# Weight blocks prepared one pair earlier, and layer one's first chains issued within attention

## The chip, the cores and the metric

One core of a Trainium2 chip runs the whole kernel. The metric is the device time of one execution in microseconds (us). Engines: TensorE (PE, matmuls), ScalarE (ACT), VectorE (DVE), GpSimd (POOL), and SyncE (SP), on whose queue all the transfers of this kernel are issued, in order.

## The reference

Causal attention with a decay, then two feed-forward layers, all in float32:

```python
scores = q @ k.T / 8 + cum[:, None] - cum[None, :]      # causal; cum = cumsum(log f)
x = softmax(scores) @ v                                  # 4 batches, 8 heads, 576 tokens, 64 wide
h = x @ w_in;  x = (h * cos(h)) @ w_out                  # 2304 x 512, hidden 2048
g = x @ w_gate; x = (g * sigmoid(g) * (x @ w_val)) @ w_out2   # hidden 1536
```

## The kernel before

Everything is unrolled, and each engine runs its instructions in program order. A matmul that needs float32 is done in three passes over rounded parts: high x high, low x high, high x low. So each weight block becomes a high and a low half, and so does each left operand.

**Attention.** The 32 heads go in 16 pairs. An order written out by hand, `SCH`, is run once per round `n`; an entry such as `N0b@2` runs operation `N0` for pair b (odd) of round `n - 2`. `S` are score matmuls (`S4` those of the last 64 tokens, both pairs of a round together), `M` adds the mask and takes the maximum on DVE, `E` is the exponential on ACT, `T` transposes on PE, `C` copies the transposed tile out of PSUM (ACT, or DVE for `C1`), `V` is the product with v, `N` (L531) multiplies by the reciprocal sums on DVE, `xo` stores the pair's result. `ld` loads a pair's q and k (576 KB, L303) into a ring of `RWB` tiles; `lv` loads v; `r` operations form the reciprocals and send them through DRAM. `XH` places three early products of layer one, `ahead(0..2)`, among the last pair's operations: `h` for hidden blocks 0, 1 and 2 of the first token chunk.

**Weight blocks.** `order` lists the blocks of 128 x 512 float64-wide words (512 KB) in the order of their use. `wd` loads block `i - 1` at pair `i` (L152), and `w1` to `w7` convert it: `w1` absolute value on ACT (L168), `w2` clamp on POOL, `w3` to `w5` shifts and merges on DVE (L172, L174, L176), `w6` and `w7` the high and low half on POOL. The first `SA` = 15 blocks (0 to 14) are done so within attention, on a ring of three raw tiles; block 14 belongs to pair 15. Four further raw tiles are loaded near the end of attention, behind `rf` of pair 15, and worked on within layer one.

**Layer one** goes over six chunks of 384 tokens and 16 hidden blocks, 96 steps. Each step runs the letters of `ORD1` = "0c152cw64cowwc": `0` twelve matmuls into h (L253), `1` n = round(h / 2 pi) on ACT (L665), `2` r = h / 2 pi - n on DVE (L667), `4` the sine on ACT (L669), `5` of the step before: product h * r on DVE (L671) and rounding to gh on ACT (L673), `6` of the step before: gl = h - gh on DVE, `w` weight work, `o` the twelve matmuls of gh and gl two steps back into four accumulator banks (L689, and L692 for the last hidden block of a chunk), `c` a piece of the second layer's weight work. After a chunk's last hidden block `o` also empties the banks: four copies on ACT (L699), or for the two chunks that are split into two halves four sums on DVE (L697). The accumulators are two tiles of two banks (`t_tile`, a ring of two), the same ring that holds attention's transposes and products.

At the seam the program order on each engine is: all of attention, then the steps of layer one from step 0 on. `h` of blocks 0 to 2 exists by then; n, r, the sine, gh and gl do not.

Of the kernel before, what the change touches and what calls it, by code (L numbers as in the profile page):

```python
# [9 lines left out]
F32 = mybir.dt.float32  # L10
F32R = mybir.dt.float32r
I32 = mybir.dt.int32
I64 = mybir.dt.int64
# [7 lines left out]
NPAIR = NH // 2  # L21
# [8 lines left out]
SA = 15  # L30
LAG = 2
PB = 6
RWB = 4
VTB = 3
PTB = 2
PST = 2
WARM = 2
TAB = 2
TAB2 = 6
RWB2 = 4  # L40
HIB = 4
CHAIN = 1
WHE = 1

XH = {("T2", 14): 0, ("T1", 15): 1, ("V0", 15): 2}
SCH = "xka@2 E21a@1 N0a@2 M11b@1 xoa@2 M10b@1 wdb@2 E00a@1 E31a@1 E01a@1 w5b@3 E30a@1 raa@1 lva@1 C3b@2 rba@1 S0b@1 T0b@2 E11b@1 wda@1 S2b@1 M01b@1 w6b@3 T2b@2 rta@1 lda@-1 S3b@1 M20b@1 M21b@1 C0b@2 C2b@2 rca@1 rda@1 E21b@1 M00b@1 M30b@1 T3a@1 M31b@1 E01b@1 w3a@2 V0b@2 w4a@2 S4@0 V1b@2 E00b@1 M40@0 E20b@1 w5a@2 w7b@3 S0a@0 M41@0 N0b@2 E30b@1 xkb@2 w6a@2 C3a@1 E31b@1 T0a@1 ldb@-1 S1a@0 M00a@0 N1b@2 rea@1 rfa@1 xob@2 E10b@1 E40@0 S2a@0 w1b@2 rab@1 rbb@1 C0a@1 E41@0 M10a@0 T2a@1 rtb@1 T1a@1 M01a@0 w7a@2 C2a@1 rcb@1 rdb@1 M11a@0 M20a@0 S3a@0 C1a@1 T1b@1 V0a@1 V1a@1 lvb@1 M21a@0 w1a@1 M30a@0 M31a@0 E11a@0 w2b@2 w3b@2 S1b@0 C1b@1 w4b@2 w2a@1 qs@-1 T3b@1 N1a@1 reb@1 rfb@1 E10a@0 E20a@0"
START = "S2a M21a M20a S3a M31a E20a M30a E21a E31a qs E30a S1a S0a M01a M00a M10a M11a E11a S4 M40 E10a M41 T1a E00a E01a C1a T0a"
DVC = ((1, 0), (1, 1))
JS = 9
# [14 lines left out]
GSUM0 = ((3, 0), (4, 1), (5, 2), (6, 3))  # L64
HAT0, LAT0 = (3, 4, 5, 6, 7, 8, 8), (4, 5, 6, 7, 8, 9, 9)
SEAM = {1: (2, 3), 6: (3, 4), 5: (4, 5), 2: (5, 6), 7: (6, 7), 3: (7, 8), 4: (8, 9)}
ORD1 = "0c152cw64cowwc"
WQ = (3, 2)
NS = 2
WS = 2  # L70
# [27 lines left out]
def body(ctx: ExitStack, tc: tile.TileContext, qk, v, f, w_in, w_out, w_gate, w_val, w_out2, mask_c, ident_c, sel_c, out):  # L98
# [48 lines left out]

    def w_load(n):
        kind, j = order[n]
        sp = stages[0] if n < SA else wraws  # L150
        raw = sp.tile([128, 512], I64, tag="wraw", name="wraw", bufs=3 if n < SA else RWB2)
        SP.dma_start(out=raw, in_=srcs[kind][j])  # L152
        wcur[n] = [raw, None]

# [122 lines left out]
    rctx = ExitStack()  # L277
    xpools[0] = rctx.enter_context(tc.tile_pool(name="xpool", bufs=1, side=SIDE_R))
    wraws = rctx.enter_context(tc.tile_pool(name="wraws", bufs=RWB2, side=SIDE_R))
    actx = ExitStack()  # L280
    ap1 = actx.enter_context(tc.tile_pool(name="ap1", bufs=1))
    ident = ap1.tile([128, 128], F32, name="ident")
# [267 lines left out]
    def op(o, q):  # L550

        if not 0 <= q < NPAIR // 2:
            return
        l = {"a": 0, "b": 1}.get(o[-1])
        if l is not None:
            o, q = o[:-1], 2 * q + l
        if (o, q) not in done:
            done.add((o, q))
            if (o, q) in XH:
                ahead(XH[o, q])  # L560
            act(o, q)
            if (o, q) == ("C0", NPAIR - 1):
                ACT.activation(out=sinp, in_=hpi, func=AF.Sin)
            if (o, q) == ("rf", NPAIR - 1):
                for k in range(RWB2):
                    w_load(SA + k)

    def act(o, i):
        k, e = o[0], int(o[-1]) if o[-1] in "01" else 0
        p = 2 * i + e  # L570
        if o[:2] == "ld":
            i > 1 and load_pair(i)
        elif o == "lv":
            prep_v(i)
        elif o == "S4":
            emit_s4(i)
        elif o[:2] == "M4":
            emit_m4(i, e)
        elif o[:2] == "E4":
            emit_e4(i, e)  # L580
        elif k == "S":
            emit_s(i, int(o[1]))
        elif k == "M":
            emit_m(p, int(o[1]))
        elif k == "E":
            emit_e(p, int(o[1]))
        elif k == "T":
            emit_t(i, int(o[1]))
        elif k == "C":
            emit_c(i, int(o[1]))  # L590
        elif k == "r":
            emit_recip(i, o[1])
        elif k == "V":
            emit_pv(i, e)
        elif k == "N":
            emit_n(i, e)
        elif o == "xo":
            emit_o(i)
        elif o == "xk":
            if i == XL:  # L600
                load_chunk(0, True)
            elif i >= XP:
                for _ in range(min(XN, len(xsplit))):
                    split_x(*xsplit.pop(0))
        elif o == "wd":
            i and w_load(i - 1)
        elif k == "w":
            i and w_step(i - 1, int(o[1]))
        elif o == "qs":
            emit_b(i)  # L610
        else:
            raise ValueError(o)
# [15 lines left out]
        mm_in(h, wt["i", j], xs[0])  # L628

    pools, hs = {}, {}  # L630
    moff = max(int(o) for _, o in sch)
    for o in START.split():
        op(o, 0)
    for n in range(NPAIR // 2 + moff):
        for o, off in sch:
            op(o, n - int(off))
    gsrc[0] = const.tile([1, 1], F32, name="gs")
    pool_round(gsrc[0], rsb[NPAIR - 1][0:1, 0:1])
    actx.close()
    wpools[1] = ctx.enter_context(tc.tile_pool(name="wb", bufs=1))  # L640
    lctx = ExitStack()
    xpools[1] = lctx.enter_context(tc.tile_pool(name="xpool2", bufs=1))
    pp = lctx.enter_context(tc.tile_pool(name="pp", bufs=1))
    mp2 = lctx.enter_context(tc.tile_pool(name="mp2", bufs=1, reuse_waits="tile"))
    mp3 = lctx.enter_context(tc.tile_pool(name="mp3", bufs=3, reuse_waits="tile"))
    stages[1] = rctx.enter_context(tc.tile_pool(name="stage2", bufs=TAB2, side=SIDE_R))
    G = {}
    acc = {}
    part = {}
    loaded = set()  # L650
    hnr = {}

    def in1(c, j, k):

        if k == 0:
            h = hs.pop((c, j), None)
            if h is None:
                h = pools["h"].tile([128, 512], F32, tag="h", name="h")[:, :CH]
                mm_in(h, wt["i", j], xs[c])
            n = mp2.tile([128, CH], I32, tag="n", name="n")  # L660
            r = mp2.tile([128, CH], F32, tag="r", name="r", bufs=2)
            hnr[c, j] = h, n, r
        h, n, r = hnr[c, j]
        if k == 1:
            ACT.activation(out=n, in_=h, func=AF.Copy, scale=INV2PI, bias=0.25)  # L665
        elif k == 2:
            DVE.scalar_tensor_tensor(out=r, in0=h, scalar=INV2PI, in1=n, op0=ALU.mult, op1=ALU.subtract)  # L667
        elif k == 4:
            ACT.activation(out=r, in_=r, func=AF.Sin, bias=hpi, scale=float(2 * np.pi))  # L669
        elif k == 5:  # L670
            DVE.tensor_tensor(out=h, in0=h, in1=r, op=ALU.mult)  # L671
            gh, gl = G[c, j] = [mp3.tile([128, CH], F32R, tag=a, name=a) for a in ("gh", "gl")]
            ACT.copy(out=gh, in_=h)  # L673
        elif k == 6:
            gh, gl = G[c, j]
            subtract(DVE, gl, h, gh)
            del hnr[c, j]

    def out1(g, j):
        c, a, b = SEG[g]  # L680
        gh, gl = G.pop((c, j))
        wo = wt["o", j]
        if j == a:
            for m in range(0, KD, 2):
                t = t_tile()
                acc[m], acc[m + 1] = t[:, 0], t[:, 1]
        for n, (q, x) in enumerate(((0, gh), (1, gh), (0, gl))) if j < b - 1 else ():
            for m in range(KD):
                PE.matmul(acc[m][:, :CH], lhsT=wo[:, q, 128 * m:128 * m + 128], rhs=x, start=(j == a and n == 0), stop=False)  # L689
        for m in range(KD) if j == b - 1 else ():  # L690
            for n, (q, x) in enumerate(((0, gh), (1, gh), (0, gl))):
                PE.matmul(acc[m][:, :CH], lhsT=wo[:, q, 128 * m:128 * m + 128], rhs=x, start=False, stop=(n == 2))  # L692
        if j == b - 1:
            o = part.pop(g)
            for m in range(KD):
                if a:
                    DVE.tensor_tensor(out=o[:, m], in0=acc[m][:, :CH], in1=o[:, m], op=ALU.add)  # L697
                else:
                    ACT.copy(out=o[:, m], in_=acc[m][:, :CH])  # L699
            SP.dma_start(out=x2[c], in_=o)  # L700

    steps = [(g, j) for g, (c, a, b) in enumerate(SEG) for j in range(a, b)]
    wpos = [SA, 2]
# [62 lines left out]
    for i in range(NCH + LAG):  # L766
        if i < NCH:
# [6 lines left out]
            if j == J1 - 7 and c + 1 not in loaded or c == 0 and j == 2 and 1 not in loaded:  # L774
                loaded.add(c + 1)
                load_chunk(c + 1, later=True)
            if i == WS:
                w_step(SA, 1)
            left = WQ[SB <= wpos[0] < SB + 24 and i % 2] if i >= WS else 0
            now[0] = i  # L780
            for k in ORD1:
                if k in "01234":
                    in1(c, j, int(k))
                elif k in "56" and i:
                    in1(SEG[steps[i - 1][0]][0], steps[i - 1][1], int(k))
                elif k == "w" and left:
                    left -= 1
                    w_next()
                elif k == "o" and i >= LAG:
                    out1(*steps[i - LAG])  # L790
                elif k == "c" and small and small[0][0] <= i:
                    small.pop(0)[1]()
            if xsplit and i >= XS:
# [309 lines left out]
```

## Time and profile before

| | |
|---|---|
| median of 3 runs (lowest, highest) | 965.83 us (965.19, 967.13) |
| the profiled execution, its own time | 966.51 us |
| its span, first to last instruction | 964.7 us |
| mean granted TensorE clock | 0.992 |
| PE busy | 944.1 us, 98% |
| DVE, ACT, POOL busy | 717.9, 510.0, 414.5 us |

Times below are from the span's start. Attention fills about the first 160 us, layer one runs to about 566, the second layer to the end. A busy PE counts pipelined matmuls; a granted clock of 1.0 is 2.4 GHz, one of 0.5 is 1.2 GHz.

### The profile page before, as it was taken

Reading aid. Unit: us, or ns where it says so; the run is one execution under the profiler, and the core shown is the slowest. Engines: PE = TensorE matmul, PEld = TensorE weight load, DVE = VectorE, ACT = ScalarE, POOL = GpSimd, SP = SyncE. Lnnn points to the kernel's source line nnn. Section 1 sums busy time; section 2 is a strip of 40 time slices with the busy share of each in tenths; the row PEclk is TensorE's granted clock in tenths of the full one; section 3 lists DMA queues with packets and bytes.
Section 4 is the critical chain, followed back from the end, with each engine's and each line's share of the span. In section 5 each row is a group of like instructions: output and inputs, shape, how many; then the busy total and the mean of one; then the engine's idle time right before and its main releaser. Section 6 shows DMA issues by size and latency. Waiting matters only on the chain.

```text
span 964.7 us, 17731 instructions
## 1 busy us (share of the span) xinstructions
PE 944.1 (98%) x6442; PEld 881.8 (91%) x6442; DVE 717.9 (74%) x1267; ACT 510.0 (53%) x1105; POOL 414.5 (43%) x389
## 2 busy tenths in 40 slices
PE   7999996999999999999999999999999999999998
PEld 4667774999999999999999999999999999988888
DVE  6788885777788788779966535766758585898884
ACT  7999993555655556556555432323324132464552
POOL 1245745423265687597791005545446455000000
PEclk9999998999999999999999999999999999999999
DMA  5577655342467759679847772326841429953431
GB/s 194 196 252 266 220 177 177 99 136 95 153 220 228 249 168 317 206 219 297 270 151 261 252 273 88 116 58 236 307 123 50 123 71 391 346 169 129 134 109 45
DMA packets 108983, 182.60 MB, mean 189 GB/s; under 512 B 8920, under 2 KB 72800, under 8 KB 108896
## 3 DMA queue, kind: packets, MB, share of 16 engines
q1 hardware_dynamic: 108896, 181.47, 56.8%
q8 instruction: 51, 0.84, 0.4%
q14 instruction: 36, 0.29, 0.1%
HBM read 118.44 MB, written 62.99 MB: 188 GB/s over the span
## 4 chain that ended last, share of the span: by engine, by line
PE 82%; DVE 5%; POOL 4%; DMA 4%; ACT 2%; issue 2%; SPq 0%; POOLq 0%; ACTq 0%; DVEq 0%
PE h L253 16%; PE t L689 15%; PE b L874 12%; PE c L874 8%; PE a L874 8%; PE b L963 5%; PE t L522 4%; PE a L963 3%; PE sB L386 2%; PE t L472 2%; DMA xl<-x 2%; PE c L963 2%; PE d L963 2%; PE sA L386 1%; PE t L692 1%
## 5 line engine op out<-in xcount | busy, mean ns | idle before, releaser
L253 PE MATMUL h<-xh,w 128*128 128x384 f32 x768 | 149.0, 335 | 0.0
L689 PE MATMUL t<-gh,w 128*128 128x384 f32 x704 | 138.4, 337 | 9.8 <-ACT gh L673 8.9
L253 PEld LDWEIGHTS h<-xh,w 128*128 128x128 f32 x768 | 134.4, 188 | 0.2
L689 PEld LDWEIGHTS t<-gh,w 128*128 128x128 f32 x704 | 124.0, 189 | 11.2 <-ACT gh L673 9.1
L874 PE MATMUL b<-c,wu 128*128 128x384 f32 x648 | 121.1, 334 | 0.0
L665 ACT ACTIVATE n<-h 128x384 int32<-128x384 f32 x96 | 47.2, 491 | 134.5 <-PE h L253 134.4
L667 DVE SCALAR_TENSOR_TENSOR r<-h,n 128x384 f32<-128x384 f32 x96 | 53.3, 555 | 80.5 <-ACT n L665 80.3
L874 PEld LDWEIGHTS b<-c,wu 128*128 128x128 f32 x648 | 113.1, 188 | 0.0
L837 POOL TENSOR_TENSOR s<-u,s 128x384 f32<-128x384 f32 x33 | 37.8, 1144 | 123.7 <-ACT s L836 110.9
L253 PE MATMUL h<-xl,w 128*128 128x384 f32 x384 | 82.1, 334 | 0.0
L874 PE MATMUL c<-c,wu 128*128 128x384 f32 x432 | 80.7, 335 | 0.0
L874 PE MATMUL a<-c,wu 128*128 128x384 f32 x432 | 80.7, 334 | 0.0
L689 PE MATMUL t<-gl,w 128*128 128x384 f32 x352 | 75.7, 336 | 0.0
L874 PEld LDWEIGHTS c<-c,wu 128*128 128x128 f32 x432 | 75.4, 188 | 0.0
L874 PEld LDWEIGHTS a<-c,wu 128*128 128x128 f32 x432 | 75.4, 188 | 0.0
L115 POOL TENSOR_TENSOR w<-ta,w 128x512 fp32r<-128x512 f32 x32 | 44.4, 1389 | 64.9 <-ACT w L190 32.3
L420 ACT ACTIVATE P<-P,mx 128x384 f32<-128x384 f32 (+3 forms) x128 | 70.4, 552 | 1.7 <-DVE mx L414 1.7
L253 PEld LDWEIGHTS h<-xl,w 128*128 128x128 f32 x384 | 67.9, 188 | 0.0
L669 ACT ACTIVATE r<-r,hpi 128x384 f32<-128x384 f32 x96 | 59.5, 620 | 14.6 <-DVE r L667 14.5
L174 DVE SCALAR_TENSOR_TENSOR ta<-wraw,ta 128x512 int32<-128x512 int32 x68 | 63.8, 938 | 0.8
L689 PEld LDWEIGHTS t<-gl,w 128*128 128x128 f32 x352 | 62.9, 189 | 0.0
L963 PE MATMUL b<-wu,c 128*128 128x256 f32 (+1 forms) x342 | 61.4, 330 | 0.2 <-DVE u L752 0.2
(149 smaller groups left out, 1973.8 us busy)
## 6 DMA issues: line engine op xcount, KB each, us to landing
wu<-wu SPq DMA_DIRECT2D x63, 512.0 KB
wraw<-in_w_out_dram SPq DMA_DIRECT2D x28, 512.0 KB
wu<-hi SPq DMA_DIRECT2D x54, 256.0 KB
gd<-g SPq DMA_DIRECT2D x72, 192.0 KB
gt<-gd SPq DMA_DIRECT2D x36, 384.0 KB
raw<-in_qk_dram SPq DMA_DIRECT2D x16, 576.0 KB
wu<-sums SPq DMA_DIRECT2D x36, 256.0 KB
xb<-x SPq DMA_DIRECT2D x24, 384.0 KB
```

Source lines behind the costliest of these rows:

```text
L115: eng.tensor_tensor(out=o, in0=a, in1=b.bitcast(F32), op=ALU.subtract)
L174: DVE.scalar_tensor_tensor(out=ta, in0=lo, scalar=29, in1=ta, op0=ALU.logical_shift_right, op1=ALU.bitwise_or)
L253: PE.matmul(ps, lhsT=w[:, a, 128 * kk:128 * kk + 128], rhs=b[:, kk], start=(n == 0), stop=(n == 3 * KD - 1))
L420: ACT.activation(out=o, in_=o, func=AF.Exp, scale=-1.0, bias=mxt[p % 8][:, t:t + 1], accum_out=smt[p // 2 % 3][:, c:c + 1])
L522: PE.matmul(ps[64 * e:64 * e + 64, o:min(w, o + KW[j])], lhsT=vt_t[i][:, j, e], rhs=PT[i][:, i % 2 ^ e, c:c + w - o], start=(j == 0), stop ...
L665: ACT.activation(out=n, in_=h, func=AF.Copy, scale=INV2PI, bias=0.25)
L667: DVE.scalar_tensor_tensor(out=r, in0=h, scalar=INV2PI, in1=n, op0=ALU.mult, op1=ALU.subtract)
L669: ACT.activation(out=r, in_=r, func=AF.Sin, bias=hpi, scale=float(2 * np.pi))
L689: PE.matmul(acc[m][:, :CH], lhsT=wo[:, q, 128 * m:128 * m + 128], rhs=x, start=(j == a and n == 0), stop=False)
L837: e.tensor_tensor(out=s, in0=C[:, 0], in1=s, op=ALU.mult)
L874: PE.matmul(d, lhsT=wu[q, i][1][:, mem, x, 128 * kt:128 * kt + 128], rhs=r, start=bool(s and n == 0), stop=(n == 5), skip_group_check=True)
L963: PE.matmul(ot[:, :w], lhsT=cmb[i][:, x, q], rhs=m[:, 256 * y:256 * y + w], start=(i in (1, 5) and n == 0), stop=(n == len(ops) - 1), skip ...
```

## The change

1. `wd` and `w1` to `w7` work on block `i` at pair `i` rather than on block `i - 1`; block 14 belongs to pair 14, and the last round of the order has nothing left to do.
2. One ring of five raw tiles holds all weight blocks; the ring of q/k tiles goes from four to three. The loads of the next blocks (15 to 19) are spread: three behind `rf` of pair 15, one each behind `w5` of blocks 13 and 14.
3. In `SCH`, `lda` goes behind `S3b`, and `ldb` from the middle of a round to behind `S3a`.
4. Layer one's chains for hidden blocks 0 and 1 (steps `0`, `1`, `2`, `4`, `5`, `6` above) are issued before `N0` of pair 15, the last of them behind `N1`; the main loop leaves out what is done. Their tiles' pools are opened ahead of attention's and stay to the end.
5. `o` stands directly behind `1` in a step; DVE's sums of the split chunks keep their old place, under a new letter `q`. The first step of block 15 moves from the start of step 2 to its first `w`.
6. The first group of a chunk goes into the four banks by twos: six matmuls into the first tile, then six into the second.

```diff
-RWB = 4
+RWB = 3
-RWB2 = 4
+RWB2 = 5
+CHAINS = ((0, 0), (0, 1), (0, 2), (1, 0), (1, 1), (0, 4), (1, 2), (0, 5), (1, 4), (0, 6), (1, 5))
+LOADS = {("rf", NPAIR - 1): (0, 1, 2), ("w5", SA - 2): (3, ), ("w5", SA - 1): (4, )}
-SCH = "... rta@1 lda@-1 S3b@1 ... T0a@1 ldb@-1 S1a@0 ... S3a@0 C1a@1 ..."
+SCH = "... rta@1 S3b@1 lda@-1 ... T0a@1 S1a@0 ... S3a@0 ldb@-1 C1a@1 ..."
-ORD1 = "0c152cw64cowwc"
+ORD1 = "0c1o52cw64cqwwc"
...
-        sp = stages[0] if n < SA else wraws
-        raw = sp.tile([128, 512], I64, tag="wraw", name="wraw", bufs=3 if n < SA else RWB2)
+        raw = wraws.tile([128, 512], I64, tag="wraw", name="wraw")
...
+            if (o, q) == ("N0", NPAIR - 1):
+                for j, k in CHAINS:
+                    in1(0, j, k)
...
-            if (o, q) == ("rf", NPAIR - 1):
-                for k in range(RWB2):
-                    w_load(SA + k)
+            if (o, q) == ("N1", NPAIR - 1):
+                in1(0, 1, 6)
+            for k in LOADS.get((o, q), ()):
+                w_load(SA + k)
...
-            i and w_load(i - 1)
+            i < SA and w_load(i)
         elif k == "w":
-            i and w_step(i - 1, int(o[1]))
+            i < SA and w_step(i, int(o[1]))
...
+        if (c, j, k) in did:
+            return
+        did.add((c, j, k))
...
-        for n, (q, x) in enumerate(((0, gh), (1, gh), (0, gl))) if j < b - 1 else ():
-            for m in range(KD):
+        for d, n, (q, x) in [(d, n, y) for d in ((0, 2) if j == a else (0, )) for n, y in enumerate(((0, gh), (1, gh), (0, gl)))] if j < b - 1 else ():
+            for m in range(d, d + 2 if j == a else KD):
...
+            if a:
+                sumq.append((c, o, dict(acc)))
+            else:
+                SP.dma_start(out=x2[c], in_=o)
...
+    def part_sums():
+        c, o, t = sumq.pop()
+        for m in range(KD):
+            DVE.tensor_tensor(out=o[:, m], in0=t[m][:, :CH], in1=o[:, m], op=ALU.add)
+        SP.dma_start(out=x2[c], in_=o)
...
-            if i == WS:
-                w_step(SA, 1)
...
+                    if wpos == [SA, 2]:
+                        w_step(SA, 1)
                     w_next()
...
+                elif k == "q" and sumq:
+                    part_sums()
```

## Rows read from the trace of the kernel before

**Rows 1.** The page, part 1: busy us, share of the span, instructions.

```profile
PE 944.1 (98%) x6442; PEld 881.8 (91%) x6442; DVE 717.9 (74%) x1267; ACT 510.0 (53%) x1105; POOL 414.5 (43%) x389
```

**Rows 2.** Windows: from:to length, busy us by engine, clock, DMA share, GB/s.

```profile
14.00:16.00 2.00, 1.95 (x22) 1.32 (x20) 1.88 (x10) 1.31 (x5) 0.00 (x0) 1.00 0.27 98
...
20.00:22.00 2.00, 1.02 (x10) 0.77 (x10) 1.78 (x7) 2.00 (x8) 0.00 (x0) 0.93 0.75 261
22.00:24.00 2.00, 2.00 (x12) 1.37 (x10) 0.76 (x4) 2.00 (x4) 0.00 (x0) 0.50 0.00 1
...
60.00:80.00 20.00, 19.88 (x260) 13.92 (x258) 17.78 (x60) 19.21 (x60) 10.79 (x11) 1.00 0.63 213
...
160.00:180.00 20.00, 11.93 (x59) 11.93 (x60) 11.11 (x22) 8.70 (x18) 8.69 (x10) 0.74 0.25 81
```

**Rows 3.** Chain of waits at the seam: start, us, what.

```profile
146.08 2.31 PE h L253 x12
...
153.02 8.09 DMA wraw<-in_w_in_dram
...
161.22 0.67 ACT ta L168
...
165.10 0.69 DVE ta L176
165.79 0.48 DVE r L667
...
166.29 0.62 ACT r L669
...
166.94 0.58 DVE h L671
...
168.07 4.10 PE t L689 x12
172.17 2.09 PE h L253 x12
```

**Rows 4.** Timeline of PE at the seam: start, us, line, form, idle before.

```profile
156.20 2.92 PE L522 MATMUL t<-pt,vt 128*64 128x256 f32 x28
168.07 2.93 PE L689 MATMUL t<-gh,w 128*128 128x384 f32 x8 [8.95 <-ACT gh L673]
```

**Rows 5.** Timeline of PE around two chunk boundaries of layer one.

```profile
367.54 1.55 PE L253 MATMUL h<-xh,w 128*128 128x384 f32 x8
...
372.30 1.55 PE L253 MATMUL h<-xh,w 128*128 128x384 f32 x8
...
435.72 1.55 PE L253 MATMUL h<-xh,w 128*128 128x384 f32 x8
...
438.56 0.61 PE L689 MATMUL t<-gh,w 128*128 128x384 f32 x2 [0.60 <-ACT part L699]
...
441.16 1.55 PE L253 MATMUL h<-xh,w 128*128 128x384 f32 x8
```

**Rows 6.** Timelines of ACT and DVE, seam and step.

```profile
155.96 0.57 ACT L494 COPY pt<-t 128x512 f32<-128x512 f32 x1
...
182.68 0.49 ACT L665 ACTIVATE n<-h 128x384 int32<-128x384 f32 x1 [1.86 <-PE h L253]
...
154.61 1.67 DVE L176 SCALAR_TENSOR_TENSOR ta<-wraw,ta 128x512 int32<-128x512 int32 x1
159.17 0.82 DVE L531 TENSOR_TENSOR xp<-t,rs 128x256 f32<-128x256 f32 x2 [2.90 <-PE t L522]
```

**Rows 7.** Chain of waits in attention: an S3 group's end, the next S4.

```profile
43.90 0.24 PE sB L389 x2
...
52.96 0.39 PE sA L397 x2
```

**Rows 8.** Timelines of SP and PE at the start of the kernel.

```profile
11.61 0.33 SPq L303 DMA_DIRECT2D raw<-in_qk_dram  x1
...
17.41 0.70 PE L397 MATMUL sA<-raw 64*64 64x288 f32 x4
```

More of the change, by code (lines that the diff above doesn't have):

```diff
@@ L43 @@
 WHE = 1
+CHAINS = ((0, 0), (0, 1), (0, 2), (1, 0), (1, 1), (0, 4), (1, 2), (0, 5), (1, 4), (0, 6), (1, 5))
+LOADS = {("rf", NPAIR - 1): (0, 1, 2), ("w5", SA - 2): (3, ), ("w5", SA - 1): (4, )}
 XH = {("T2", 14): 0, ("T1", 15): 1, ("V0", 15): 2}
-SCH = "xka@2 E21a@1 N0a@2 M11b@1 xoa@2 M10b@1 wdb@2 E00a@1 E31a@1 E01a@1 w5b@3 E30a@1 raa@1 lva@1 C3b@2 rba@1 S0b@1 T0b@2 E11b@1 wda@1 S2b@1 M01b@1 w6b@3 T2b@2 rta@1 lda@-1 S3b@1 M20b@1 M21b@1 C0b@2 C2b@2 rca@1 rda@1 E21b@1 M00b@1 M30b@1 T3a@1 M31b@1 E01b@1 w3a@2 V0b@2 w4a@2 S4@0 V1b@2 E00b@1 M40@0 E20b@1 w5a@2 w7b@3 S0a@0 M41@0 N0b@2 E30b@1 xkb@2 w6a@2 C3a@1 E31b@1 T0a@1 ldb@-1 S1a@0 M00a@0 N1b@2 rea@1 rfa@1 xob@2 E10b@1 E40@0 S2a@0 w1b@2 rab@1 rbb@1 C0a@1 E41@0 M10a@0 T2a@1 rtb@1 T1a@1 M01a@0 w7a@2 C2a@1 rcb@1 rdb@1 M11a@0 M20a@0 S3a@0 C1a@1 T1b@1 V0a@1 V1a@1 lvb@1 M21a@0 w1a@1 M30a@0 M31a@0 E11a@0 w2b@2 w3b@2 S1b@0 C1b@1 w4b@2 w2a@1 qs@-1 T3b@1 N1a@1 reb@1 rfb@1 E10a@0 E20a@0"
+SCH = "xka@2 E21a@1 N0a@2 M11b@1 xoa@2 M10b@1 wdb@2 E00a@1 E31a@1 E01a@1 w5b@3 E30a@1 raa@1 lva@1 C3b@2 rba@1 S0b@1 T0b@2 E11b@1 wda@1 S2b@1 M01b@1 w6b@3 T2b@2 rta@1 S3b@1 lda@-1 M20b@1 M21b@1 C0b@2 C2b@2 rca@1 rda@1 E21b@1 M00b@1 M30b@1 T3a@1 M31b@1 E01b@1 w3a@2 V0b@2 w4a@2 S4@0 V1b@2 E00b@1 M40@0 E20b@1 w5a@2 w7b@3 S0a@0 M41@0 N0b@2 E30b@1 xkb@2 w6a@2 C3a@1 E31b@1 T0a@1 S1a@0 M00a@0 N1b@2 rea@1 rfa@1 xob@2 E10b@1 E40@0 S2a@0 w1b@2 rab@1 rbb@1 C0a@1 E41@0 M10a@0 T2a@1 rtb@1 T1a@1 M01a@0 w7a@2 C2a@1 rcb@1 rdb@1 M11a@0 M20a@0 S3a@0 ldb@-1 C1a@1 T1b@1 V0a@1 V1a@1 lvb@1 M21a@0 w1a@1 M30a@0 M31a@0 E11a@0 w2b@2 w3b@2 S1b@0 C1b@1 w4b@2 w2a@1 qs@-1 T3b@1 N1a@1 reb@1 rfb@1 E10a@0 E20a@0"
 START = "S2a M21a M20a S3a M31a E20a M30a E21a E31a qs E30a S1a S0a M01a M00a M10a M11a E11a S4 M40 E10a M41 T1a E00a E01a C1a T0a"
@@ L279, in body @@
     wraws = rctx.enter_context(tc.tile_pool(name="wraws", bufs=RWB2, side=SIDE_R))
+    mp2 = ctx.enter_context(tc.tile_pool(name="mp2", bufs=1, reuse_waits="tile"))
+    mp3 = ctx.enter_context(tc.tile_pool(name="mp3", bufs=3, reuse_waits="tile"))
     actx = ExitStack()
@@ L630, in body @@
     pools, hs = {}, {}
[L631 to L651, printed above, removed]
+    G, hnr, did = {}, {}, set()
     def in1(c, j, k):
+        if (c, j, k) in did:
+            return
+        did.add((c, j, k))
         if k == 0:
@@ L677, in in1 @@
             del hnr[c, j]
+    moff = max(int(o) for _, o in sch)
+    for o in START.split():
+        op(o, 0)
+    for n in range(NPAIR // 2 + moff):
+        for o, off in sch:
+            op(o, n - int(off))
+    gsrc[0] = const.tile([1, 1], F32, name="gs")
+    pool_round(gsrc[0], rsb[NPAIR - 1][0:1, 0:1])
+    actx.close()
+    wpools[1] = ctx.enter_context(tc.tile_pool(name="wb", bufs=1))
+    lctx = ExitStack()
+    xpools[1] = lctx.enter_context(tc.tile_pool(name="xpool2", bufs=1))
+    pp = lctx.enter_context(tc.tile_pool(name="pp", bufs=1))
+    stages[1] = rctx.enter_context(tc.tile_pool(name="stage2", bufs=TAB2, side=SIDE_R))
+    acc = {}
+    part = {}
+    loaded = set()
     def out1(g, j):
@@ L694, in out1 @@
             o = part.pop(g)
[L695 to L700, printed above, removed]
+            for m in range(KD) if not a else ():
+                ACT.copy(out=o[:, m], in_=acc[m][:, :CH])
+            if a:
+                sumq.append((c, o, dict(acc)))
+            else:
+                SP.dma_start(out=x2[c], in_=o)
+    sumq = []
+    def part_sums():
[3 more added lines that the diff above has]
+        SP.dma_start(out=x2[c], in_=o)
     steps = [(g, j) for g, (c, a, b) in enumerate(SEG) for j in range(a, b)]
```

## The prediction

> **What bounds the kernel now.** I read the page first: TensorE (PE) is busy 98% of the span [rows 1], so a change can win only where PE stands still, or runs at the lower of its two clock levels. The windows say where. In the middle of attention PE is busy 19.88 of 20 us, with ScalarE (ACT) close behind at 19.21; the one large hole is 160 to 180 us, the seam from attention to layer one, with PE busy 11.93 of 20 and a mean granted clock of 0.74 [rows 2]. Then I followed the chain of waits through the seam. It leaves PE, runs 8.09 us through the load of a raw weight block issued at 153.02, through that block's steps (ACT at 161.22, then GpSimd and VectorE), and only at 165.79 reaches layer one's first chain: r on VectorE (DVE), the sine on ACT, the product on DVE, the rounding to gh on ACT, and PE at 168.07 [rows 3]. This is weight block 14, the last that attention prepares. Layer one has no use for it yet: DVE works in order, and block 14's steps stand ahead of r. PE's timeline gives the price: the last attention product ends at 156.20 + 2.92 = 159.12, and PE then waits 8.95 us for gh [rows 4]. The next twelve matmuls take 4.10 us where the following group of the same shape takes 2.09 [rows 3]: the clock is at 1.2 GHz after the gap, which costs 2.0 us more. So the seam costs 8.95 + 2.0 = 10.95 us.
>
> The last view is PE's timeline in layer one, where one step (twelve matmuls into h, twelve out of gh and gl) should take 2 x 2.08 = 4.16 us. Two steps do not: 367.54 to 372.30 is 4.76 us, and 435.72 to 441.16 is 5.44 us, with PE waiting for ACT's L699 [rows 5]. L699 copies the finished sums of one token chunk out of the accumulator banks, and stands behind the sine and the weight casts in ACT's order. Those losses are 0.60 + 1.28 = 1.88 us.
>
> **The seam.** Blocks move forward by one pair: block 14's load takes the slot that block 13's has now, in the round before, and its last three DVE steps the slots of block 13's. So the load that the chain waits for is gone, and DVE's weight work ends where block 13's ends now, at 154.61 + 1.67 = 156.28 [rows 6]. Layer one's chains for the first two column blocks are now issued before DVE's last two attention products (N0 and N1 of pair 15). Their h tiles are there: the second ends at 146.08 + 2.31 = 148.39 [rows 3]. What sets the start is ACT's order: the last copy of attention ends at 155.96 + 0.57 = 156.53 [rows 6]. The rounding n takes 0.49 [rows 6], so r can start at about 157.05. From the start of r to PE's first matmul took 168.07 - 165.79 = 2.28 us [rows 3]; so PE starts at about 159.35, 0.23 us after its last attention product.
>
> This is where the two-bank order counts. The first accumulator tile takes over a slot that was read out by 156.53; the second takes the slot of pair 15's attention product, which is free only after N0 and N1. These two (0.82 us together [rows 6]) now stand on DVE behind the second chain's product. Counting the rows' durations on: gh of chain 0 ready at 159.3, sine of chain 1 to 159.95, its product to 160.5, N0 and N1 to 161.35. PE's first six matmuls (two banks) run 159.35 to 160.4, the other six wait until 161.4, another 1.0 us. gl of chain 1 follows at 161.9, some 3 us before its use. The new idle time is 0.23 + 1.0, about 1.25 us, in two pieces; I take it that the clock then stays at 2.4 GHz. Seam: 1.25 - 10.95 = -9.7 us. Bounds: if nothing is left idle, -10.95; if the clock still falls, 2.0 less is won, -7.7.
>
> **The chunk boundaries.** The L699 copies move ahead of gh, the sine and the casts, directly behind n. The four copies then follow the four sums as these end, and the accumulators are free some 0.5 us after PE's last sum, while PE has a 2.08 us group of h in between. gh of the other chain comes later by up to the four copies, and gl with it, but gl is used only after the first four matmuls of the next group. Both waits should go: -1.88 us. Lower bound 0, if the wait turns into one for gl. DVE's sums of the split chunks keep their place (they are only issued by another letter of the step's order), so they cost nothing; the cover is the same group of h.
>
> **Attention.** Round one gets a block's first steps, and the last round loses one. ACT does 0.67 us more (a block's first step, the row at 161.22 in [rows 3]) before the end of attention. PE is the bound there, and ACT has 0.79 us free in 20 [rows 2], so I take 0; without that cover it is +0.67. DVE's and GpSimd's extra steps in round two only make it like the later rounds.
>
> The raw q/k ring falls from four tiles to three, so two loads wait on SyncE (SP) for a slot. The odd pair's load waits for the last score group of the pair that it replaces. Behind it in SP's queue stand the v tile, the reciprocal rows and an attention store, none wanted for some microseconds. In a round this group ends at 43.90 + 0.24 = 44.14, and the new pair is first read at 52.96 [rows 7]: 8.8 us for 576 KB. The first time is tighter: pair 3 can be issued only when the slot is read out, where pair 4's load stands now, at 11.61, and is read at 17.41 [rows 8]. Pair 4's transfer, issued there now, is down to 98 GB/s in the window 14 to 16 [rows 2], so it lands by about 16: no stall. The even pair's load now waits for a score group just ahead of it and holds the reciprocal stores back by some tenths of a microsecond, with microseconds of room before the rows are used. Term 0; bound below.
>
> Pools for the chains stand outside attention's memory, so the chains wait for no slot. The five-block ring and the first step of block 15, moved inside its step, change no order on PE: term 0, covered by the PE-bound steps of layer one.
>
> **Sum.** -9.7 - 1.9 + 0 = -11.6 us. The profiled execution took 966.51 us, its span 964.7; it becomes 954.9. It is 0.68 above the median of the runs shown, 965.83, so the forecast for the median is 954.2 us.
>
> **The clock.** At the start of the kernel PE was busy 1.02 of 2 us in 20 to 22, so no gap there was longer than 0.98, and in 22 to 24 the clock stood at 1.2 GHz [rows 2]. So broken work can drop the clock here too. The Trainium skill (TensorE: Matmul & The Clock Gate, "A second HAM failure mode: psum-queue depth-cycling") says that short idle times between groups of matmuls, when accumulator banks are cycled, can let the clock fall and rise again; that speaks against splitting the first sums by banks. The trace at 20 to 24 agrees with that; no row shows it for full 128 x 128 groups.
>
> **Rivals.** (1) The clock falls in the seam all the same: two waits instead of one, each after only six matmuls. +2.0: 956.2. Against it: the waits are together 1.25 us, before and after them PE is busy throughout. (2) The chain comes late: ACT or DVE meet a slow step ahead of it (DVE's last weight step took 1.67 us [rows 6], the same step at 165.10 only 0.69 [rows 3]), or one of the two chains delays N0 and N1 further. Two to three microseconds of idle time come back: 956 to 957.5. (3) The boundary waits become waits for gl, because DVE is nearly full in that stretch: +1.88, 956.1. (4) The other side: the ring of three starves attention. Seven odd pairs wait for their load; the 11.6 us are eaten up if each lands 11.6 / 7 = 1.66 us late, 10.5 us after its issue. The longest load in the rows took 8.09 us [rows 3], with four blocks queued ahead of it; here nearly nothing is ahead. At 3 us late each it is 7 x 3 = 21 us: 965.8 - 11.6 + 21 = 975. (5) The order change hides nothing, because something else holds gh: then only the boundaries are won, 964.
>
> **How the numbers follow.** My forecast, 952.8 to 955.6: 0.60. Rival 1: 0.10; rival 2: 0.12; rival 3: 0.08 (all three faster). Rivals 4 and 5 and other losses in attention: 0.05, of which 0.03 slower, 0.01 within 0.2% and 0.01 faster. Better than 952.8 (no idle left, or a lucky clock at the start): 0.05. The likeliest gives 954.2; the range 952.4 to 957.4 takes in rivals 1 to 3 and the lower bound of the seam. Runs before spread over 0.2%, about what can be told from no change; faster by more than that has 0.96, the same 0.01, slower 0.03.
>
> **What would show it.** Right: no load of a weight block in the chain at the seam; PE's wait for gh under 1 us, a second one of about 1 us that ends on DVE's xp (L531); the first twelve matmuls of layer one in about 2 us of work; full steps of 4.16 us at the two chunk boundaries; attention's last product still at about 159. Wrong: waits of PE on raw q/k tiles once a round, a clock of 0.5 behind the seam, or attention's end later than 160.

## The result and the profile after

The changed kernel took 955.46 us (median of 6 runs, 953.68 to 957.54), the kernel before, run beside it, 966.23 (6 runs, 965.19 to 967.55): a ratio of 0.9888, 95% interval 0.9872 to 0.9904. The forecast was 954.2, its range 952.4 to 957.4. The profiled execution took 955.27 us with a span of 953.5, against 964.7 before. Its span divides at three matmuls: the end of attention's last product, the first group into h behind layer one's first sums, and layer two's first group.

| us | before | after | difference | predicted |
|---|---|---|---|---|
| start to the end of attention's last product | 159.12 | 158.59 | -0.53 | 0 |
| from there to the first h group (the seam) | 12.89 | 3.63 | -9.26 | -9.7 |
| from there to layer two (layer one) | 393.95 | 392.60 | -1.35 | -1.9 |
| layer two | 398.74 | 398.68 | -0.06 | 0 |
| span | 964.7 | 953.5 | -11.2 | -11.6 |

The page's line of busy time, and windows (from:to length, busy us by engine, clock, DMA share, GB/s), which answer to [rows 1] and [rows 2]:

```profile
PE 940.7 (99%) x6442; PEld 878.9 (92%) x6442; DVE 718.6 (75%) x1267; ACT 510.9 (54%) x1105; POOL 417.0 (44%) x389
```

```profile
22.00:24.00 2.00, 1.57 (x22) 1.07 (x18) 1.44 (x9) 2.00 (x4) 0.00 (x0) 1.00 0.42 148
...
60.00:80.00 20.00, 19.94 (x262) 13.98 (x260) 17.77 (x59) 19.21 (x61) 11.02 (x11) 1.00 0.68 230
...
160.00:180.00 20.00, 19.39 (x112) 19.10 (x111) 17.34 (x32) 11.19 (x22) 9.36 (x10) 1.00 0.41 125
```

The hole at 160 to 180 is closed: 19.39 us busy instead of 11.93, at a clock of 1.00 instead of 0.74. The clock also stands at 1.00 in 22 to 24, where it stood at 0.50; of that more below. The chain of waits through the seam, which answers to [rows 3] (start, us, what):

```profile
155.98 0.40 ACT n L655
...
156.41 0.57 DVE r L657
...
157.00 0.50 ACT n L655
...
157.52 0.56 DVE r L657
158.08 0.52 DVE h L661
...
160.12 0.82 DVE xp L534 x2
...
161.08 1.30 PE t L696 x6
162.39 2.09 PE h L254 x12
```

No load and no weight step stands in it any more. It starts behind ACT's last copy of attention, as forecast, but it goes through ACT's n twice: the second n starts only when the first r has ended. PE's and ACT's timelines there (start, us, line, form, idle before and what ended it) answer to [rows 4] and [rows 6]:

```profile
155.66 2.93 PE L525 MATMUL t<-pt,vt 128*64 128x256 f32 x28
159.16 0.97 PE L696 MATMUL t<-gh,w 128*128 128x384 f32 x4 [0.57 <-ACT gh L663]
159.96 0.51 PE L696 MATMUL t<-gl,w 128*128 128x384 f32 x2
161.08 0.94 PE L696 MATMUL t<-gh,w 128*128 128x384 f32 x4 [0.61 <-DVE xp L534]
161.86 0.52 PE L696 MATMUL t<-gl,w 128*128 128x384 f32 x2
162.22 1.56 PE L254 MATMUL h<-xh,w 128*128 128x384 f32 x8
```

```profile
157.00 0.49 ACT L655 ACTIVATE n<-h 128x384 int32<-128x384 f32 x1 [0.62 <-DVE r L657]
157.38 0.61 ACT L659 ACTIVATE r<-r,hpi 128x384 f32<-128x384 f32 x1
158.62 0.48 ACT L663 CAST gh<-h 128x384 fp32r<-128x384 f32 x1 [0.63 <-DVE h L661]
```

PE's wait of 8.95 us for gh is 0.57. The second wait, for xp, is 0.61. The clock stays at 2.4 GHz throughout.

PE's timeline in layer one, which answers to [rows 5]:

```profile
357.92 1.55 PE L254 MATMUL h<-xh,w 128*128 128x384 f32 x8
...
362.08 1.55 PE L254 MATMUL h<-xh,w 128*128 128x384 f32 x8
...
422.61 0.51 PE L699 MATMUL t<-gh,w 128*128 128x384 f32 x2
423.79 0.44 PE L699 MATMUL t<-gl,w 128*128 128x384 f32 x1 [0.68 <-DVE gl L117]
...
425.66 1.55 PE L254 MATMUL h<-xh,w 128*128 128x384 f32 x8
...
427.74 0.86 PE L696 MATMUL t<-gh,w 128*128 128x384 f32 x4
```

The first boundary is a step of 362.08 - 357.92 = 4.16 us. At the second PE no longer waits for the copies: the group of h takes its 2.08 us (425.66 to 427.74), and the whole step 4.36 (425.66 to 430.02). But one step earlier, in the chunk's last sums, PE waits 0.68 us for gl, and the group takes 3.05 us instead of 2.08. The kernel before has the same wait at the same place, and the prediction did not list it:

```profile
433.88 0.44 PE L692 MATMUL t<-gl,w 128*128 128x384 f32 x1 [0.69 <-DVE gl L115]
```

In attention two products wait that did not before. From PE's list of waits (what was waited for, total, times, longest) and SP's timeline:

```profile
PE t L525 <- DMA vt<-in_v_dram: 0.6, 1, 0.6
...
PE t L525 <- ACT P L423: 0.6, 1, 0.6
```

```profile
113.88 0.36 SPq L306 DMA_DIRECT2D raw<-in_qk_dram  x1
114.28 0.46 SPq L310 DMA_DIRECT2D vt<-in_v_dram  x1
```

The first in time, at 103.49, is for ACT; the other, at 121.31, is for a v tile whose load was issued at 114.28, directly behind a q/k load.

### The profile page after: what moved, and what is told of

It reads as the page before. It is cut to its first block, busy times and chain, and to the rows that moved or that the text cites. A ratio compares the mean times of both kernels' runs of the same rounds, so it can differ in the third digit from the quotient of the medians.

```text
span 953.5 us, 17728 instructions
## 1 busy us (share of the span) xinstructions
PE 940.7 (99%) x6442; PEld 878.9 (92%) x6442; DVE 718.6 (75%) x1267; ACT 510.9 (54%) x1105; POOL 417.0 (44%) x389
## 4 chain that ended last, share of the span: by engine, by line
PE 90%; DVE 4%; DMA 2%; ACT 2%; issue 1%; SPq 0%; DVEq 0%; ACTq 0%
PE h L254 20%; PE t L696 19%; PE b L891 12%; PE c L891 8%; PE a L891 8%; PE b L980 5%; PE t L525 4%; PE a L980 3%; PE sB L389 2%; PE t L699 2%; PE t L475 2%; PE c L980 2%; PE d L980 2%; PE sA L389 1%; DVE P L417 1%
```

## The experiments

My theory: early chains plus early blocks make the seam, and each alone would leave a part of it; the two-bank order and the step order are worth about a microsecond each. The rivals are those of the prediction. Times are medians of 4 runs, each with its ratio to the kernel before on the same chip; single runs of one kernel spread by some 2 us, so terms below 1 us are read from the stretch in the profile that they belong to. No run takes back the rings of tiles or the places of `lda` and `ldb` by themselves.

**1. The chains back behind attention.** The blocks stay early.

```diff
-            if (o, q) == ("N0", NPAIR - 1):
-                for j, k in CHAINS:
-                    in1(0, j, k)
-            if (o, q) == ("N1", NPAIR - 1):
-                in1(0, 1, 6)
```

> The changed kernel without the early chains: blocks one pair earlier, the rings, the new step order and the two-bank first groups stay; n, r, sine, gh and gl of hidden blocks 0 and 1 are issued by the main loop again. Theory A (the late load of block 14 and its steps in DVE's order were most of the seam, the early place of the chains the rest): no block load in the chain of waits; r of chain 0 starts behind N0 and N1 at about 159.4, gh follows 2.3 to 2.8 us later, so PE waits about 3.3 us after attention's last product instead of 0.57 + 0.61; +2 us against the changed kernel if the clock stays, +4 if it falls: about 957 to 960. Rival B (the early issue is what counts, the block's place does not): the wait stays near 9 us and the time near 964.

958.06 us (956.68 to 959.02), ratio 0.9912 (0.9893 to 0.9931). PE and DVE in the seam:

```profile
162.15 0.98 PE L691 MATMUL t<-gh,w 128*128 128x384 f32 x4 [3.14 <-ACT gh L658]
...
164.36 1.55 PE L254 MATMUL h<-xh,w 128*128 128x384 f32 x8
```

```profile
159.05 0.82 DVE L534 TENSOR_TENSOR xp<-t,rs 128x256 f32<-128x256 f32 x2 [2.91 <-PE t L525]
159.79 0.55 DVE L652 SCALAR_TENSOR_TENSOR r<-h,n 128x384 f32<-128x384 f32 x1
```

DVE stood idle for 2.91 us in front of N0, which waits for PE's last product, and r stands behind N0. That is what the early chains use. The seam is 164.36 - 159.00 = 5.36 us, 1.7 more than with them. Rival 5 (964 us: something else holds gh) falls: with the chains back behind attention, 7.5 of the 9.26 us are still there (12.89 - 5.36). In this profile the clock did not fall after the gap of 3.14 us: it is 1.00 from 157 to 166.

**2. The blocks back at their old pairs.** The chains stay early; the loads of the blocks are issued later, four ahead.

```diff
-LOADS = {("rf", NPAIR - 1): (0, 1, 2), ("w5", SA - 2): (3, ), ("w5", SA - 1): (4, )}
+LOADS = {("rf", NPAIR - 1): (0, 1), ("w5", SA - 1): (2, ), ("w5", SA): (3, )}
-            i < SA and w_load(i)
+            i and w_load(i - 1)
...
-            i < SA and w_step(i, int(o[1]))
+            i and w_step(i - 1, int(o[1]))
...
-        if k == 5 and n + RWB2 < len(order):
-            w_load(n + RWB2)
+        if k == 5 and n + RWB2 - 1 < len(order):
+            w_load(n + RWB2 - 1)
```

> The changed kernel with the weight blocks back at their old pairs (block 14 at pair 15, loaded at about 152.6 and used until about 165), on the ring of five with loads four ahead; the early chains stay. Theory A: chains 0 and 1 stand ahead of block 14 in DVE's order, so the first two groups of layer one start as in the changed kernel (waits of 0.6 and 0.6 us); the third chain's r stands behind block 14's steps at about 165.5, gl of it is ready at about 168.5, just when PE wants it: +0 to +1 us against the changed kernel, about 955.5 to 956.5. Rival B (the late load must be gone, or PE only waits one or two groups later): the wait comes back at the third group, 3 us or more, 959 or later.

957.54 us (956.07 to 958.86), ratio 0.9907 (0.9887 to 0.9927). The first two waits are those of the changed kernel, 0.56 and 0.61 us, and the seam 3.61. The loss comes at the third group, by PE's timeline, ACT's and a window:

```profile
168.03 0.86 PE L254 MATMUL h<-xl,w 128*128 128x384 f32 x4
170.95 2.26 PE L696 MATMUL t<-gh,w 128*128 128x384 f32 x8 [2.06 <-ACT gh L663]
```

```profile
167.60 0.66 ACT L169 ACTIVATE ta<-wraw 128x512 f32<-128x512 f32 x1 [5.64 <-POOL w L117]
168.17 0.60 ACT L659 ACTIVATE r<-r,hpi 128x384 f32<-128x384 f32 x1
```

```profile
170.90:174.40 3.50, 3.45 (x13) 3.45 (x14) 3.47 (x7) 3.17 (x7) 1.60 (x3) 0.62 1.04 391
```

ACT's first step of block 15 waits 5.64 us for memory that block 14 holds until GpSimd's last step, and the third chain's sine stands behind it, though its r was ready at 165.41 + 0.55 on DVE. The Trainium skill (TensorE: Matmul & The Clock Gate, "Architectural detail: the array is 16× 32×32, not 1× 128×128") says that ScalarE's and VectorE's queues are strictly first in, first out; these two rows agree. After PE's 2.06 us of waiting the mean clock is 0.62. That is this execution, the longest of the four; the shortest, 956.07 us, has a mean clock of 1.000 over its whole span, from which such a window would take 0.001, so the fall does not come each time. The expectation of theory A missed: the block's lateness is not hidden, it shows at the third group, where rival B put it, but with 2.06 us instead of 3 or more. So early chains alone also close most of the seam, and the two parts overlap: the kernel without the one gains 7.8 us (965.83 to 958.06), without the other 8.3 (to 957.54), with both 10.8.

**3. The first sums into four banks at once**, as before.

```diff
-for d in ((0, 2) if j == a else (0, )) ...
-            for m in range(d, d + 2 if j == a else KD):
+for d in (0, ) ...
+            for m in range(KD):
```

> The changed kernel with the first group of each chunk over four banks again (the order by twos undone). Theory A: PE issues two matmuls and then waits for N0 and N1 with ten still to go instead of six: the group ends 0.7 us later, +0.7 us in all, nothing at the chunk boundaries, where the copies now end 1.3 us before their use. Rival B: the second wait is not for the slot of attention's product, then no difference.

956.33 us (954.05 to 958.59), ratio 0.9891 (0.9862 to 0.992).

```profile
160.66 1.30 PE L696 MATMUL t<-gh,w 128*128 128x384 f32 x6 [1.31 <-DVE xp L534]
```

The wait for xp is 1.31 instead of 0.61 and the seam 4.35 instead of 3.63: 0.7 us, as expected. That nothing would change at the chunk boundaries was half wrong. At 264.42, where a split chunk's sums are read out by DVE, a group lost 0.57 us (PE waiting for part, L714); with the banks by twos the step there lost 0.17 (262.07 to 266.40). At the two boundaries of [rows 5] nothing is lost (358.59 to 362.75, and the second here), so the new step order alone removes both of those waits:

```profile
427.29 1.55 PE L254 MATMUL h<-xh,w 128*128 128x384 f32 x8
...
431.45 1.55 PE L254 MATMUL h<-xh,w 128*128 128x384 f32 x8
```

**4. The old order of a step.**

```diff
-ORD1 = "0c1o52cw64cqwwc"
+ORD1 = "0c152cw64coqwwc"
```

> The changed kernel with the accumulator's copies at their old place in a step (behind the sine and the casts). Theory A (the boundary losses came from that place): the two boundary steps of chunks 2 to 3 and 3 to 4 lose again, but less than the 0.6 and 1.28 us of before, since the first six matmuls want two of the four banks only: +0.4 to +1.4 us. Rival B: the losses of before came from DVE being late there, then they are the same as in the changed kernel and the time too.

955.69 us (955.05 to 956.25), ratio 0.9888 (0.9871 to 0.9906).

```profile
427.93 0.98 PE L696 MATMUL t<-gh,w 128*128 128x384 f32 x4 [0.60 <-ACT part L703]
```

The wait for the copies is back at the second boundary, with its 0.76 us; the first boundary still takes 4.16 us. Layer one took 393.56 us, 0.96 more than in the changed kernel's profile, 0.70 of it at this boundary (425.09 to 430.15 is 5.06 us, against 4.36). The median, 955.69 against 955.46 us, doesn't show it. The order's worth rests on these stretches alone.

**5. The changed kernel again**, for the comparisons to come.

> The changed kernel itself, for comparison on the same chip: 955.5 us, with attention's last product ending within a microsecond of 158.6 (its first third is a microsecond or so shorter or longer by whether the clock falls near 21 us).

955.52 us (954.64 to 956.11), ratio 0.988 (0.9865 to 0.9895). Its profile has no wait for v at all; the last product ends at 157.69, the seam is 3.62, layer one 392.80.

**6. The v load ahead of the q/k load** of the odd pair: in `SCH`, `lvb@1` goes directly before `ldb@-1`.

> The changed kernel with the odd pair's v load issued ahead of the odd pair's q/k load instead of behind it. Theory A (the ring of three put 576 KB and a wait ahead of the v load, and the two waits of 0.6 us at 103.5 and 121.3 are its price): no wait of an attention product on v, attention 0.2 to 0.9 us shorter: about 954.7 us. Rival B (the transfers as a whole are late there, whatever their order): the waits stay, or move to the q/k tiles, time unchanged.

955.09 us (954.04 to 955.6), ratio 0.9875 (0.986 to 0.989). No wait for v, the last product ends at 157.75. But run 5 on the same chip had none either, so this tells nothing apart. Over the thirteen profiles of this study a product waits for v by 0.6 us in one execution and by 0.2 in two, and in none before the change.

**7. The chains one after the other.** N0 stands between them, so that nothing of the second chain is in front of the first.

```diff
-CHAINS = ((0, 0), (0, 1), (0, 2), (1, 0), (1, 1), (0, 4), (1, 2), (0, 5), (1, 4), (0, 6), (1, 5))
+CHAINS = ((0, 0), (0, 1), (0, 2), (0, 4), (0, 5), (0, 6))
...
             if (o, q) == ("N1", NPAIR - 1):
-                in1(0, 1, 6)
+                for k in (0, 1, 2, 4, 5, 6):
+                    in1(0, 1, k)
```

> The changed kernel with the chain of hidden block 0 issued whole before N0 of pair 15, and that of block 1 whole behind N1. Theory A (the second rounding waits for the first r, since they share one tile, and the sine of chain 0 stands behind it; N0 and N1 stand behind chain 1's product): first wait 0.57 us to about 0.15, second wait 0.61 to about 0.25, so 0.8 to 1.2 us less: about 954.4 us. Rival B: chain 1 is then too late for the second group, and the time comes back there.

953.5 us (952.69 to 954.84), ratio 0.9857 (0.9841 to 0.9874). PE and DVE:

```profile
158.31 0.97 PE L697 MATMUL t<-gh,w 128*128 128x384 f32 x4 [0.19 <-ACT gh L664]
159.12 0.52 PE L697 MATMUL t<-gl,w 128*128 128x384 f32 x2
159.73 0.94 PE L697 MATMUL t<-gh,w 128*128 128x384 f32 x4
160.50 0.51 PE L697 MATMUL t<-gl,w 128*128 128x384 f32 x2
160.85 1.55 PE L254 MATMUL h<-xh,w 128*128 128x384 f32 x8
```

```profile
158.77 0.81 DVE L534 TENSOR_TENSOR xp<-t,rs 128x256 f32<-128x256 f32 x2
```

N0 and N1 start 0.7 us after the last product's end instead of 1.5, and the first chain waits for nothing of the second. The seam is 160.85 - 158.12 = 2.73 us, 0.9 less than in the changed kernel, as expected; rival B's loss behind it did not come.

**8. Both, 6 and 7.**

> Both: v ahead of q/k, and chain by chain. Theory A: the two add up, 1.0 to 2.0 us less than the changed kernel, 953.5 to 954.5 us. Rival B: one of them only, or neither: 954.5 to 955.5.

953.61 us (952.94 to 955.73), ratio 0.9865 (0.9849 to 0.9881): seam 2.74. The time alone would fit theory A, but run 7 has it without the loads' new order, which adds nothing.

**9. Chains one after the other, and the last sums by twos of banks**, against the wait for gl at 422.

```diff
-        for m in range(KD) if j == b - 1 else ():
-            for n, (q, x) in enumerate(((0, gh), (1, gh), (0, gl))):
+        for d, n, (q, x) in [(d, n, y) for d in (0, 2) for n, y in enumerate(((0, gh), (1, gh), (0, gl)))] if j == b - 1 else ():
+            for m in range(d, d + 2):
```

> The kernel with the chains one after the other, and besides, in the last hidden block of a chunk, the sums go by twos of banks (four matmuls of gh, two of gl, and again) instead of bank by bank, so that gl is wanted 0.35 us later. Theory A: the one wait left at a chunk boundary (at about 422 us, 0.7 us for gl, 0.97 us lost with what follows) shrinks by about 0.35; the copies of the accumulators start 0.35 later and are still done within the 2.08 us group of h. Layer one 0.2 to 0.4 us shorter than with the chains one after the other alone (392.7), time 953.2. Rival B: ACT's copies end too late and the next chunk's first sums wait instead: layer one the same or longer.

954.19 us (953.74 to 955.05), ratio 0.9873 (0.9853 to 0.9893).

```profile
426.36 0.86 PE L697 MATMUL t<-gh,w 128*128 128x384 f32 x4
427.43 0.61 PE L697 MATMUL t<-gl,w 128*128 128x384 f32 x2 [0.21 <-DVE gl L117]
```

The last sums take their 2.08 us now, and the next group loses 0.51: by PE's row, to gl again and not to the copies. Layer one took 391.63 us.

**10. The chains one after the other, again**, beside run 9.

> The kernel with the chains one after the other, unchanged, on the same chip as the two others: seam 2.7 us, layer one 392.7, about 953.5 to 954; a comparison for both.

953.68 us (952.66 to 954.36), ratio 0.9868 (0.9851 to 0.9886), seam 160.61 - 157.88 = 2.73, layer one 391.49. In this execution the wait at the last sums cost 0.13 us, where run 7's profile has 0.96. So the loss at 422 varies from one execution to the next, and run 9 can't be judged by one profile; its time shows no gain.

**11. Memory of its own for the second chain's n.** A second tile for n in the whole of layer one does not fit: the next pool then wants 28 KB of a partition, and 26.75 are left. So only the second chain's n gets another place, a tile of probabilities that attention no longer uses.

```diff
-            n = mp2.tile([128, CH], I32, tag="n", name="n")
+            n = Ps[2][:, :CH].bitcast(I32) if (c, j) == (0, 1) else mp2.tile([128, CH], I32, tag="n", name="n")
```

> The changed kernel with n of the second chain in memory of its own (a tile of probabilities that attention no longer uses), and nothing else; two tiles for n in the whole of layer one take more memory than there is. Theory A: at the seam ACT's n of the second chain waits 0.62 us for r of the first only because both use one tile, and the first sine stands behind that n. Then n follows at once, the first sine starts some 0.4 us earlier, and the first six matmuls of the seam start after some 0.2 us of idle time instead of 0.57. The second six still wait for N0 and N1; the seam (end of attention's last product to the first h group behind the first sums, 3.63 us in the changed kernel) becomes about 3.2, time about 0.4 lower, 955. Rival B: it is the order as such that costs, and the tile only moves the wait: seam unchanged at 3.6.

955.29 us (954.62 to 956.27), ratio 0.9897 (0.9881 to 0.9914). ACT and PE:

```profile
156.76 0.49 ACT L655 ACTIVATE P<-h 128x384 int32<-128x384 f32 x1
157.50 0.62 ACT L659 ACTIVATE r<-r,hpi 128x384 f32<-128x384 f32 x1 [0.25 <-DVE r L657]
```

```profile
159.28 0.97 PE L696 MATMUL t<-gh,w 128*128 128x384 f32 x4 [0.21 <-ACT gh L663]
...
161.21 0.93 PE L696 MATMUL t<-gh,w 128*128 128x384 f32 x4 [0.60 <-DVE xp L534]
...
162.33 1.55 PE L254 MATMUL h<-xh,w 128*128 128x384 f32 x8
```

The second n follows the first without a wait, the first sine waits for its own r alone, and PE's first wait is 0.21 us, as the prediction had it (0.23). The seam is 162.33 - 159.07 = 3.26. The shared tile for n cost the 0.37 us, and theory A holds for the stretch; the median (ratio 0.9897, beside 0.9888 for the changed kernel) doesn't show so small a term. The other 0.5 us that run 7 wins are, by subtraction, N0 and N1 standing behind the second chain: their wait of 0.60 us is here still, and in run 7 it is not.

## Why the prediction was right, point by point

**The seam** (-9.7 forecast, -9.26 measured) was right in mechanism. Its cause was the load of block 14 ahead of r, and both the moved block and the early chain were needed for the whole of it (runs 1 and 2). The step "so PE starts at about 159.35, 0.23 us after its last attention product" was mis-sized: 0.57 in place of 0.23. It counted r and sine of the first chain as if nothing stood between, but the order issues n of the second chain first, and that n has to wait for r, because there is one tile for n; the sine stands behind it on ACT. Run 11 shows that this is all of the difference. The second piece, "another 1.0 us", measured 0.61 as PE's wait, because it counts from a start that was itself later, and because the first six matmuls took 1.31 us and not 1.05; N0 and N1 ended at 160.93, 2.3 us after the last product, as the count had it (161.35 against 159.12, 2.2). From PE's start to the first h group it is 3.06 us (159.16 to 162.22), about what the forecast gives (2.05 to the second six, and 1.04 for them). So the 0.44 us that the seam falls short are 0.34 for the later start, and for the rest mainly the seam of before: its 12.89 us are 10.81 above twelve matmuls at 2.08, and the sum took 10.95. The bank split won the 0.7 us that run 3 takes back.

**The clock** stayed at its higher level over the two waits, as I took it; rival 1 did not come. In all ten profiles with the banks by twos and the chains early, the window from 157 to 166 us has a mean granted clock of 1.00; run 2's fall came only behind a third wait, of 2.06 us. The Trainium skill's rule (TensorE: Matmul & The Clock Gate, "A second HAM failure mode: psum-queue depth-cycling"), which spoke for that rival, finds no case in this seam. Nor is the fall at 22 to 24, which the prediction took as agreeing with it, steady: PE's waits up to 21 us are the same in the changed kernel's profile (0.34 and 0.86 us, against 0.34 and 0.85), and the clock there stays at 1.00.

**The chunk boundaries** (-1.88 forecast). The copies' wait is gone at both. The two steps of [rows 5] lost 0.60 and 1.28 us against 4.16; after it the losses are 0 and 0.20 (427.74 to 430.02), so -1.7 there. Layer one as a whole won 1.35: two small losses are new, 0.17 us at the boundary of a split chunk (262.07 to 266.40), which the forecast put at nothing, and 0.21 at 416.16 to 420.53. Runs 3 and 4 show that the order of the step is what removes the wait at the second boundary; at the first either the order or the banks by twos is enough. The 0.20 left at the second is the price of the twos: gl is wanted there after four matmuls instead of eight, and DVE's gl is ready only at 428.44; run 3, with all four banks at once, loses nothing there. What the forecast overlooked is the wait for gl at 422, which the kernel before has too, at 433.88: in the changed kernel DVE is busy 13.90 of the 14 us from 416 to 430, and gl stands behind a weight step of 1.11 us there. Rival 3 named that engine rightly, but this wait is an old one; of the one that it meant only the 0.20 us came.

**Attention** (0 forecast, -0.53 measured) is the term that came out near by two things that the sum did not hold, and that is luck. At 22 to 24 the clock stood at 1.00, where [rows 2] have 0.50. By the round that follows (its first S4 group at 34.13 instead of 35.52) that is 1.39 us. It isn't the change's doing: of the thirteen profiles, that of before included, six show 0.5 in this window and seven 1.0, with both among kernels that differ only in layer one (0.5 in run 9, 1.0 in run 10). Run 11 is one:

```profile
22.00:24.00 2.00, 2.00 (x12) 1.29 (x10) 0.67 (x4) 2.00 (x4) 0.00 (x0) 0.50 0.35 124
```

Against it stand 0.86 us, given back between that round and the end, among them the two waits of a product in attention. The step "the v tile, the reciprocal rows and an attention store, none wanted for some microseconds" was the weak one: the v tile took 6.9 us to land and was late by 0.6 once. In the next profile of the same kernel (run 5) neither wait was there, so this is no steady price; attention's last product ended at 157.69 there, 1.43 us earlier than before, which is what the clock gave. Compared at the same clock, the forecast of 0 holds within about half a microsecond: in the five experiments with 0.5 in this window that product ended between 158.87 and 159.64, against 159.12 before. Rival 4, the starved ring of three, did not come: no PE wait on raw once a round, and S4 groups follow each other by 17.4 us as before, but for the two rounds with these waits (18.0 and 17.8). The forecast of the median lies 1.26 us below the measured one: 0.40 of it is the kernel before, which took 966.23 in these runs instead of 965.83. The rest is that the medians lie 10.77 us apart, not 11.6. The two profiles lie 11.2 apart: the seam gave 0.44 and layer one 0.5 less than forecast, attention 0.53 more. The remaining 0.4 is within what runs of one kernel differ by.

**The better version.** The chains one after the other (runs 7 and 10) beat both kernels: 953.5 and 953.68 us, against 955.52 for the changed kernel beside run 7. The seam explains 0.9 of these 2.0 us, seen three times as 2.73 or 2.74 (run 8 has it too); the other 1.1 I can't place, and with runs that spread by 2 us it may not be there. Three stretches change from one execution of a kernel to the next and can make up that spread: the clock at 22 to 24 (some 1.3 us), the wait for gl at 422 (0.13 or 0.96 in runs 10 and 7), and layer two, which took 398.70 us in run 10 and 399.56 in run 7.

## What to carry to other kernels

At a seam between two stages, look for what stands ahead of the first needed instruction in each engine's program order: here a weight block that nobody wanted yet cost 9 us, and the cure was to move either side of it. When two chains are interleaved to start early, count each buffer that they share: one tile for n, and DVE's last steps put behind the second chain, gave back 0.9 us of what the interleaving should have won. Read a term below 1 us from its own stretch of the profile, and look at a second execution before giving it a cause.

## What I had not expected of the hardware

A longer gap doesn't always move the clock, nor a shorter one leave it alone. PE's wait of 3.14 us in run 1 was followed by groups at the full pace; in run 2 a wait of 2.06 us, some ten microseconds after two shorter ones, was followed by a window at 0.62; before the change 8.95 us were followed by 1.2 GHz, as [rows 3] show. And at 22 to 24 us nearly the same program ran at 0.5 in six profiles and at 1.0 in seven, worth some 1.3 us each time. What decides it the runs don't show.

Layer two has two paces as well, at a granted clock of 1.00 in both. In its last part a group of twelve matmuls takes 2.10 us in six of the thirteen profiles and 2.12 in seven, and layer two as a whole 398.6 to 398.7 or 399.5 to 399.6. Runs 7 and 10, one kernel, are one of each, so it is no effect of a change; its cause is open.
